# DeltaNet and a SiLU layer on one core: an earlier place for chunk 1's queries, a later one for three weight-narrowing steps

## The chip, the cores and the metric

The kernel runs on one core of one Trainium2 chip. The metric is the device time of one execution in microseconds (us). Five engines matter: PE multiplies matrices, DVE and ACT and POOL do elementwise work, and SP only issues DMAs. Each has its own stream of instructions; the streams meet through semaphores.

## The reference, cut to what matters

The input is a DeltaNet attention block (4 batches, 8 heads, 768 tokens, head size 48) followed by a SiLU layer with two weight matrices, 384 x 2048 and 2048 x 384.

```python
k_n = k / (norm(k) + 1e-6)
for t in range(768):
    y[:, :, t] = q[:, :, t] @ state                    # output reads the old state
    v_old = state.T @ k_n[:, :, t]
    state = state + beta[t] * outer(k_n[:, :, t], v[:, :, t] - v_old)
x = y.transpose(0, 2, 1, 3).reshape(3072, 384)
h = x @ w_in
out = (h / (1 + exp(-h))) @ w_out
```

The inputs come as 64-bit numbers; a float64 word arrives as two 32-bit words.

## The kernel before, in words

**Tiling.** The 768 tokens are cut into six chunks of 128, and each chunk into two halves of 64. Within a chunk the recurrence is solved as a small triangular system: `invert_first` inverts 16 x 16 corners of it on DVE for chunk 0, and the generator `joins(0)` then puts the corners together into 32 x 32 and 64 x 64 inverses with PE, in ten stages (`corner` twice, `turned` twice, `straight` and the first `merge_half` for each half of the batches, and the second `merge_half` twice). Each stage is a run of small matmuls into PSUM followed by copies of the result into SBUF, one half by ACT (`by_act`, L565) and one by DVE (`by_dve`, L568). After the stages `solve(0)` goes on with `inner` (L859), whose first result, `pz` of the first batch half, ACT copies into a slab in `sums_of_w`, and DVE copies into `z`. `first_outputs` (L905) multiplies from that slab.

**Weights.** The first weight matrix comes in eight pieces of 256 columns, 0 to 7. A piece is loaded as raw 64-bit words by `fetch_w_in` in three DMAs of 256 KB (L291), and is then narrowed to 32-bit floats by `narrow` in four instructions: two on ACT (L231, an Abs; L232, an Identity that rewrites the raw words in place), two on DVE (L236, L240), and an integer add on POOL (L244). A piece is a `Piece` object in a queue: `begin` issues its two ACT instructions; of the three counted steps of `fill`, the first issues nothing more, the second L236, the third L240 and L244. `begin_next` begins the first piece of the queue that has not begun, if its load has been issued.

**What sets the order.** The order on each engine is written out by hand: `pin` ties every instruction to the one before it on its engine. `joins` takes a list `between` with one entry for each of its ten stages, which is called when that stage has been issued; `none` does nothing, `sized` issues a POOL multiply and begins piece 1, `filled(n)` is n steps of `fill`. After the ten stages a script of letters is read: `s` is the next step of `solve`, `f` one step of `fill`, `b` is `begin_next`, `T` and `q` turn one batch of chunk 1's keys or queries with PE (`turn`, L521, which copies them to `stage` with ACT, L531 and L535), `j` goes on with the second half's stages, `r` runs one step of the SiLU layer (`hidden`, L1068).

**Loads.** All loads of this stretch are issued by SP, in the order of `in_line`. `pace` makes the next DMA wait for a given instruction. `deep` makes each DMA of a group wait for the one issued two before it to have landed, so that two are under way. An entry of `pace` takes the place of the `deep` wait for the DMA that it is put on. Chunk 1's queries (`load_q(1)`) are six DMAs, two of 192 KB and four of 96 KB (L142), into the tile `sums_of_g`; pieces 2 to 5 are loaded into `w_outs`, which the second weights take over later.

The entry `fetched`, called when the second `corner` stage has been issued, sends off the loads of this stretch:

```python
linked(fetch_w_in, 2, of=pins[seen_on])   # pace on the last DVE instruction so far (L743)
deep(load_q, 1)
for i in (3, 4, 5, 6):
    deep(fetch_w_in, i)
```

Of the kernel before, what the change touches and what calls it, by code (L numbers as in the profile page):

```python
# [19 lines left out]
def kernel(  # L20
# [11 lines left out]
    B, H, S, D = q.shape  # L32
# [8 lines left out]
    T = 32  # L41
# [36 lines left out]
    pins = {}  # L78

    def pin(op):  # L80

        engine = op.ins.engine
        if engine in pins:
            behind(op, pins[engine])
        pins[engine] = op
        return op

    line, pace, depth = [], [], []
# [21 lines left out]
    def together(*parts):  # L110
        for _ in zip_longest(*parts):
            pass
# [58 lines left out]
    def linked(fetch, *args, of=None):  # L171

        pace.append(of or line[-1])
        fetch(*args)

    def deep(fetch, *args):

        depth.append(True)
        fetch(*args)
        depth.pop()  # L180
# [22 lines left out]
    seen_on = pin(nc.vector.memset(seen[:], 0.0)).ins.engine  # L203
# [9 lines left out]
    for e in range(2):  # L213
        for g in range(2):
            to, of = slice(HH * e + HH // 2 * g, HH * e + HH // 2 * (g + 1)), slice(HH // 2 * g, HH // 2 * (g + 1))
# [596 lines left out]
    def merge_half(g, hf, second):  # L812

        y = ys[0][:, g]
        pms = [bank(room, "px" if second else "py") for room in (A, CC)]
        for i in range(HH // 2):
            for e in range(2):
                n, k = 2 * i + e, hf ^ e ^ g
                even, odd = slice(W * k, W * k + T), slice(W * k + T, W * (k + 1))
                if second:  # L820
                    to, left, right = even, y[odd, n, :], xis[g][odd, n, T:W]
                else:
                    left = aps[0, g][0][even, n // H, n % H, T:W]
                    to, right = odd, xes[0][even, g * HH + n, :]
                yield pin(nc.tensor.matmul(
                    pms[k][to, T * i : T * (i + 1)], lhsT=left, rhs=right, start=True, stop=True
                ))
        for k, by in enumerate((by_act, by_dve)):
            e, half = hf ^ k ^ g, slice(W * k, W * k + T) if second else slice(W * k + T, W * (k + 1))
            of = pms[k][half, 0 : HH // 2 * T].rearrange("p (h t) -> p h t", t=T)  # L830
            by(xis[g][half, e::2, T:W] if second else y[half, e::2, :], of)
# [442 lines left out]
    def fill(n):  # L1274

        for _ in range(n):
            if not queue:
                return
            piece = queue[0]
            piece.begin()  # L1280
            piece.done += 1
            if piece.done > 1:
                next(piece.steps)
            if piece.done == 3:
                narrowed.append(piece.name)
                queue.popleft()
                for i in freed:
                    fetch_w_out(i)
                freed[:] = {
                    ("in", 4): [0], ("in", 5): [1], ("in", 7): [4], ("out", 2): [5], ("out", 3): [6], ("out", 4): [7]  # L1290
                }.get(piece.name, [])
                if eager and queue and queue[0].name in raws:
                    soon.append(queue[0])
            elif eager and piece.done == 1 and len(queue) > 1 and queue[1].name in raws:
                soon.append(queue[1])
# [108 lines left out]
    def joins(hf, between=()):  # L1404

        for stage in (
            corner(0, hf), corner(1, hf), turned(0, hf), turned(1, hf), straight(0, hf), merge_half(0, hf, False),
            straight(1, hf), merge_half(1, hf, False), merge_half(0, hf, True), merge_half(1, hf, True),
        ):
            yield from stage  # L1410
            for what in between[:1]:
                for one in what if isinstance(what, tuple) else (what,):
                    one()
            between = between[1:]
# [4 lines left out]
    def filled(n):  # L1419
        return lambda: fill(n)  # L1420

    def fetched():
        linked(fetch_w_in, 2, of=pins[seen_on])
        deep(load_q, 1)
        for i in (3, 4, 5, 6):
            deep(fetch_w_in, i)

    def sized():
# [3 lines left out]
    def none():  # L1432
        pass

    together(joins(0, [none, fetched, none, sized, filled(2), none, filled(1), none, begin_next, none]))

    pieces = chained(hidden(0, 0), hidden(0, 1), project())

# [132 lines left out]
                pieces = chained(feed_forward(1, 0), feed_forward(1, 1))  # L1571

    for text in (
        "s f s f T f q T s q T j5 j4 j8 j8 f j5 f q r T j20 j5 j8 j4 j16 j5 j4 b r q r f j4 j4 f W7 r b j4 f2 j4 j4 j32 r f e j6 j6 b j8 j4 f j4 j20 f j4 r j4 j99 l h f2 b l s w2 f r2 l p r s l w3 r p r l p f l2 f l3 b l f l2 s l f l p l3 r l3 s l f l r l2 p f s2 l2 H f l4 f r2 f p2 v l g G r i p i p r2 f i i2 r i r i b l i r f r i r b r2 i b b b i2 r2 i2 f b i5 r6 f r f r i2 r2 f r i r f r f i4 f i b r2 i3 b f b f r i r i f k r f r z i b r s r2 t z s b r2 b s m2 r5 t f t m f t m2 r s t m r b s b m r m2 s r m r m r c m2 s m r m t b m2 s m2 b m f m2 t r t m3 r m s m",
    ):
        script(text)
    for c in range(1, NCH):
# [59 lines left out]
```

## Time and profile before

| what | before |
|---|---|
| median of three runs | 641.72 us (639.18 to 643.24) |
| the profiled execution's own time | 639.7 us |
| its span | 638.0 us |
| PE busy | 621.5 us, 97% of the span |
| DVE, ACT, POOL busy | 399.1, 216.7, 94.2 us |
| mean granted PE clock | 0.986 |

The span is the time between the first and the last instruction of the profiled execution; 1.7 us of its own time lie around it. Where the profile says "idle before <- X", X is the thing that came last of what the instruction waited for. The granted clock is the share of full speed that the chip gave to PE. A row of SP's timeline is the issue of DMAs, not their movement; a DMA's landing is told in the landing summaries, or by the next issue that waited for it.

### The profile page before, as it was taken

To read this page: it belongs to the slowest core of one execution; us is meant where nothing else is said; L and a number is where in the kernel's file an instruction comes from. 1 tells how busy PE (TensorE), PEld (TensorE's weight loads), DVE (VectorE), ACT (ScalarE), POOL (GpSimd) and SP (SyncE) were. 2 spreads that over 40 slices of the span, in tenths; PEclk is the share of its full clock that TensorE was granted. 3 is DMA by queue.
4 is the path that set the end of the run, shared out by engine and by line. 5 is a ranking of instruction groups with operands and counts; after the bars stand their busy time and mean duration, and the time that the engine had idled before them with its cause. 6 is when DMAs were issued, how large, how long until landed. Compare 5 with 4: busy or idle time off the path is not lost.

```text
span 638.0 us, 21886 instructions
## 1 busy us (share of the span) xinstructions
PE 621.5 (97%) x9650; PEld 547.8 (86%) x9650; DVE 399.1 (63%) x902; ACT 216.7 (34%) x510; POOL 94.2 (15%) x95
## 2 busy tenths in 40 slices
PE   8789999999999999999999999999999999999997
PEld 5678788666789989989989989989999989989997
DVE  6855879998765975654976564986564964212112
ACT  3565665152251122451122451122451122441110
POOL 5423531246010020020020010020001000000000
PEclk9968999999999999999999999999999999999999
DMA  7845554160459242369242259233173033100101
GB/s 152 182 124 179 179 128 100 52 149 3 102 120 163 57 89 24 83 126 147 39 107 29 69 122 160 56 88 37 43 142 72 19 83 34 39 15 1 26 0 26
DMA packets 141694, 53.68 MB, mean 84 GB/s; under 512 B 113296, under 2 KB 135056, under 8 KB 141600
## 3 DMA queue, kind: packets, MB, share of 16 engines
q1 hardware_dynamic: 141120, 51.62, 39.6%
q8 instruction: 76, 1.25, 0.9%
q10 hardware_dynamic: 480, 0.67, 0.3%
q14 instruction: 18, 0.15, 0.1%
HBM read 39.62 MB, written 10.49 MB: 79 GB/s over the span
## 4 chain that ended last, share of the span: by engine, by line
PE 95%; DVE 3%; issue 1%; POOL 0%; ACT 0%; DVEq 0%; POOLq 0%
PE phid L1068 40%; PE px L1175 17%; PE py L1175 13%; PE po L1103 7%; PE pa L550 3%; PE pz L859 2%; PE ph L847 2%; PE pyc L940 2%; PE pyc L927 2%; PE pu L879 2%; PE pt L521 1%; PE px L801 1%; PE py L801 1%; PE pw L349 1%; PE pl L752 1%
## 5 line engine op out<-in xcount | busy, mean ns | idle before, releaser
L1068 PE MATMUL phid<-xT,w_in 128*128 128x256 f32 x1152 | 258.7, 383 | 0.1
L1068 PEld LDWEIGHTS phid<-xT,w_in 128*128 128x128 f32 x1152 | 217.1, 191 | 30.6 <-issue 1.0
L1078 ACT ACTIVATE gT<-phid 128x512 f32<-128x512 f32 x88 | 52.6, 598 | 145.0 <-PE phid L1068 140.7
L648 DVE SCALAR_TENSOR_TENSOR rank<-g,step,x 128x31 f32<-128x31 f32 (+15 forms) x124 | 49.7, 401 | 35.8 <-DMA g<-blocks 32.4
L1157 DVE TENSOR_TENSOR sums_of_g<-gT 128x384 f32<-128x384 f32 (+1 forms) x60 | 29.7, 514 | 56.5 <-ACT gT L1078 45.9
L1175 PE MATMUL py<-w_out,sums_of_g 128*128 128x192 f32 x320 | 56.8, 329 | 0.0
L1175 PE MATMUL px<-sums_of_w,sums_of_g 128*128 128x192 f32 x320 | 56.6, 329 | 0.0
L1175 PEld LDWEIGHTS px<-sums_of_w,sums_of_g 128*128 128x128 f32 x320 | 52.2, 190 | 0.5
L1175 PEld LDWEIGHTS py<-w_out,sums_of_g 128*128 128x128 f32 x320 | 52.2, 190 | 0.4
L653 DVE TENSOR_TENSOR x<-x,rank 128x31 f32<-128x31 f32 (+15 forms) x124 | 42.5, 343 | 4.3
L488 POOL TENSOR_TENSOR vf<-vf,n_slot 128x768 f32<-128x768 f32 x10 | 15.2, 1538 | 168.4 <-DMA vf<-in_v_dram 168.4
L886 DVE TENSOR_TENSOR state<-state,pu 48x384 f32<-48x384 f32 x44 | 24.3, 552 | 23.2 <-PE pu L879 22.3
L565 ACT COPY xT<-pyc 48x128 f32<-48x128 f32 (+2 forms) x120 | 31.2, 260 | 1.6
L509 DVE STREAM_TRANSPOSE kq<-stage 128x512 f32<-128x512 f32 x28 | 28.3, 1114 | 3.6 <-DMA stage<-in_q_dram 3.5
L1175 PE MATMUL py<-w_out,gT 128*128 128x192 f32 x160 | 28.4, 329 | 0.0
L1175 PE MATMUL px<-sums_of_w,gT 128*128 128x192 f32 x160 | 28.4, 329 | 0.0
L1175 PE MATMUL px<-w_out,gT 128*128 128x192 f32 x160 | 28.0, 327 | 0.0
L859 PEld LDWEIGHTS pz<-vf,xi 64*64 64x64 f32 x768 | 25.1, 142 | 3.2 <-issue 2.2
L571 POOL COPY g<-x 64x256 f32<-64x256 f32 x4 | 5.0, 1247 | 152.3 <-DVE x L656 152.3
L1175 PEld LDWEIGHTS px<-w_out,gT 128*128 128x128 f32 x160 | 26.4, 190 | 0.5
L859 PE MATMUL pz<-vf,xi 64*64 64x48 f32 x768 | 26.8, 226 | 0.0
L1175 PEld LDWEIGHTS py<-w_out,gT 128*128 128x128 f32 x160 | 26.1, 190 | 0.3
(202 smaller groups left out, 827.7 us busy)
## 6 DMA issues: line engine op xcount, KB each, us to landing
vf<-in_v_dram SPq DMA_DIRECT2D x48, 96.0 KB, 2.7
out_dram<-o SPq DMA_DIRECT2D x42, 96.0 KB, 2.2
w_out<-in_moe_w_in_dram SPq DMA_DIRECT2D x12, 256.0 KB, 3.3
sums_of_w<-in_moe_w_out_dram SPq DMA_DIRECT2D x8, 384.0 KB, 3.7
blocks<-ap SPq DMA_DIRECT2D x40, 64.0 KB, 1.9
kb<-in_k_dram SPq DMA_DIRECT2D x12, 192.0 KB, 4.4
kb<-in_k_dram SPq DMA_DIRECT2D x24, 96.0 KB, 4.6
raw<-in_moe_w_in_dram SPq DMA_DIRECT2D x9, 256.0 KB, 3.5
```

What stands on the lines that cost most here:

```text
L509: pin(nc.vector.transpose(out=kqs[c, b][:, :, j, :].rearrange("p a (i m) -> p a m i", i=T), in_=src.rearrange("p a (m d) -> p a m d", d=D) ...
L550: pin(nc.tensor.matmul(pa[e][half, p * n * W : (p + 1) * n * W], lhsT=kq[rows, p, 0, half], rhs=kq[rows, p, js[0] : js[-1] + 1, half], sta ...
L565: return pin(nc.scalar.copy(to, of))
L648: pin(nc.vector.scalar_tensor_tensor(out=tv, in0=g[:, 0:m, m : m + 1].to_broadcast([P, m, n]), scalar=step[:, m : m + 1], in1=x[:, m : m + ...
L653: yield pin(nc.vector.tensor_tensor(out=x[:, 0:m, m:T], in0=x[:, 0:m, m:T], in1=tv, op=ALU.add))
L859: yield pin(nc.tensor.matmul(pz[rows, n * D : (n + 1) * D], lhsT=xis[g][rows, u * H + 2 * p + e, :], rhs=vfs[c][rows, hf, g * HB + u, p, : ...
L886: pin(nc.vector.tensor_tensor(out=to, in0=to, in1=by_heads(pu[of]), op=ALU.add))
L1068: pin(nc.tensor.matmul(ph[:, j * GT : (j + 1) * GT], lhsT=w_in[:, a, (2 * f + j) * P : (2 * f + j + 1) * P], rhs=xTs[c, hf][:, a, :], star ...
L1078: pin(nc.scalar.activation(out=hidden_of(c, hf, f), in_=ph[:], func=ACTF.Silu, scale=-0.5 if in_blocks(c) else 0.5))
L1103: pin(nc.tensor.matmul(pos[i][:, 0:DM], lhsT=hidden_of(0, hf, f // 2)[:, at : at + C], rhs=w_outs[f // HFF][:, f % HFF, :], start=(f == 0) ...
L1157: pin(nc.vector.tensor_tensor(out=sums_of_g[:, k, fs], in0=of[0], in1=of[1], op=op))
L1175: pin(nc.tensor.matmul(to, lhsT=at, rhs=quarter(f, *b) if isinstance(b, tuple) else sums_of_w[b][:, f], start=start and f == 0, stop=f == ...
```

## The change: what it does

In `fetched`, chunk 1's queries are issued first, with the pace on the same DVE instruction, and piece 2 behind them as the first of the `deep` pieces. In the list of `joins(0)`, the third step of `fill` for piece 0 (L240 on DVE, L244 on POOL) goes from behind the second `straight` stage to behind the last stage, and `begin_next`, which there begins piece 2 (L231 and L232 on ACT), leaves the list. It comes back as a `b` at the head of the script, ahead of the first step of `solve(0)`.

```diff
     def fetched():
-        linked(fetch_w_in, 2, of=pins[seen_on])
+        pace.append(pins[seen_on])
         deep(load_q, 1)
-        for i in (3, 4, 5, 6):
+        for i in (2, 3, 4, 5, 6):
             deep(fetch_w_in, i)
...
-    together(joins(0, [none, fetched, none, sized, filled(2), none, filled(1), none, begin_next, none]))
+    together(joins(0, [none, fetched, none, sized, filled(2), none, none, none, none, filled(1)]))
...
     for text in (
-        "s f s f T f q T s q T j5 ...
+        "b s f s f T f q T s q T j5 ...
```

More of the change, by code (lines that the diff above doesn't have):

```diff
@@ L1573 @@
     for text in (
-        "s f s f T f q T s q T j5 j4 j8 j8 f j5 f q r T j20 j5 j8 j4 j16 j5 j4 b r q r f j4 j4 f W7 r b j4 f2 j4 j4 j32 r f e j6 j6 b j8 j4 f j4 j20 f j4 r j4 j99 l h f2 b l s w2 f r2 l p r s l w3 r p r l p f l2 f l3 b l f l2 s l f l p l3 r l3 s l f l r l2 p f s2 l2 H f l4 f r2 f p2 v l g G r i p i p r2 f i i2 r i r i b l i r f r i r b r2 i b b b i2 r2 i2 f b i5 r6 f r f r i2 r2 f r i r f r f i4 f i b r2 i3 b f b f r i r i f k r f r z i b r s r2 t z s b r2 b s m2 r5 t f t m f t m2 r s t m r b s b m r m2 s r m r m r c m2 s m r m t b m2 s m2 b m f m2 t r t m3 r m s m",
+        "b s f s f T f q T s q T j5 j4 j8 j8 f j5 f q r T j20 j5 j8 j4 j16 j5 j4 b r q r f j4 j4 f W7 r b j4 f2 j4 j4 j32 r f e j6 j6 b j8 j4 f j4 j20 f j4 r j4 j99 l h f2 b l s w2 f r2 l p r s l w3 r p r l p f l2 f l3 b l f l2 s l f l p l3 r l3 s l f l r l2 p f s2 l2 H f l4 f r2 f p2 v l g G r i p i p r2 f i i2 r i r i b l i r f r i r b r2 i b b b i2 r2 i2 f b i5 r6 f r f r i2 r2 f r i r f r f i4 f i b r2 i3 b f b f r i r i f k r f r z i b r s r2 t z s b r2 b s m2 r5 t f t m f t m2 r s t m r b s b m r m2 s r m r m r c m2 s m r m t b m2 s m2 b m f m2 t r t m3 r m s m",
     ):
```

## The prediction

> **What bounds the kernel now.** I read the page first, then the windows, to see where PE is not busy.
>
> ```profile
> span 638.0 us, 21886 instructions
> ...
> PE 621.5 (97%) x9650; PEld 547.8 (86%) x9650; DVE 399.1 (63%) x902; ACT 216.7 (34%) x510; POOL 94.2 (15%) x95
> ...
> PE 95%; DVE 3%; issue 1%; POOL 0%; ACT 0%; DVEq 0%; POOLq 0%
> ```
> ```profile
> 26.00:43.00 17.00, 12.72 (x514) 12.02 (x518) 9.57 (x18) 8.22 (x16) 8.72 (x7) 0.61 0.60 156
> ...
> 160.00:200.00 40.00, 38.28 (x583) 31.99 (x582) 23.60 (x58) 14.55 (x39) 4.02 (x4) 1.00 0.59 122
> 200.00:300.00 100.00, 100.00 (x1472) 92.52 (x1471) 67.14 (x163) 29.53 (x76) 8.44 (x9) 1.00 0.52 91
> ```
>
> In a row of windows the columns are the stretch, its length, busy us of PE, PEld, DVE, ACT and POOL, the granted clock, the DMA share and GB/s. PE is the bound: 621.5 of 638.0 us, 95% of the chain, and full from 200 to 300. The edit lies in 26 to 48 us, where PE is busy for 12.72 of 17.00 us in the first stretch and has a granted clock of 0.61. What PE loses there comes back only from later idle time, and there is little: 1.72 us in 160 to 200, none in 200 to 300. So the question is how much later or earlier PE leaves this stretch.
>
> The chain of waits in this stretch, and then ACT, DVE and PE in order of time:
>
> ```profile
> 36.33 0.43 DVE xi L568
> ...
> 36.79 0.96 DVE w_in L240
> ...
> 37.78 0.44 DVE xe_y L568
> ...
> 38.60 1.06 PE px L825 x31
> 39.67 3.47 PE pz L859 x62
> ```
> ```profile
> 37.58 0.88 ACT L231 ACTIVATE w_in<-w_out 128x768 f32<-128x768 f32 x1
> 38.37 0.97 ACT L232 ACTIVATE w_out<-w_out,plus 128x768 int32<-128x768 uint32 x1
> 39.70 0.36 ACT L565 COPY xi<-px 32x256 f32<-32x256 f32 x1 [0.37 <-PE px L825]
> 41.64 0.48 ACT L565 COPY sums_of_w<-pz 128x384 f32<-128x384 f32 x1 [1.58 <-PE pz L859]
> ```
> ```profile
> 42.16 0.56 DVE L568 COPY z<-pz 128x384 f32<-128x384 f32 x1 [2.09 <-ACT sums_of_w L565]
> ...
> 43.01 1.14 PE L905 MATMUL py<-ap,sums_of_w 64*64 64x64 f32 x46
> ...
> 44.57 0.60 PE L521 MATMUL pt<-ident,sums_of_g 128*128 128x128 f32 x4
> ```
>
> Piece 0's L240 (0.96 us) stands in the chain, between two DVE copies of the joins: that is a real delay. Piece 2's two ACT steps run from 37.58 to 39.34, 1.76 us, and have not waited for their data. After the joins, PE's `first_outputs` (L905) starts at 43.01 from the slab that ACT's copy at 41.64 writes.
>
> **The change part by part.**
>
> *Piece 0's L240 and L244 behind the joins.* DVE no longer holds the `xe_y` copy: it can follow the `xi` copies at 36.8 instead of 37.78, so the last `px` matmuls and all behind them come 0.96 us earlier. L240 and POOL's add then run from about 39, when DVE is idle (2.09 us before 42.16). Their result is needed by the first `hidden` matmuls, which stand behind all of L905 and most of the eight turns of chunk 1: these hide them, and without that cover they would cost their own time. Worth -0.96 us, if nothing else gates `first_outputs`. ACT's copies lose nothing by L244, and POOL has nothing else queued there.
>
> *The loads.* SP's issues, one row each (start, duration of the issue):
>
> ```profile
> 27.41 0.44 SPq L291 DMA_DIRECT2D raw<-in_moe_w_in_dram  x1
> 29.22 0.81 SPq L291 DMA_DIRECT2D w_out<-in_moe_w_in_dram  x2
> 33.37 0.38 SPq L142 DMA_DIRECT2D sums_of_g<-in_q_dram  x1
> 33.98 0.61 SPq L142 DMA_DIRECT2D sums_of_g<-in_q_dram  x1
> 36.57 0.60 SPq L142 DMA_DIRECT2D sums_of_g<-in_q_dram  x1
> 37.27 0.58 SPq L142 DMA_DIRECT2D sums_of_g<-in_q_dram  x1
> 39.55 0.60 SPq L142 DMA_DIRECT2D sums_of_g<-in_q_dram  x1
> 40.38 1.44 SPq L142 DMA_DIRECT2D sums_of_g<-in_q_dram  x1
> 42.62 0.35 SPq L291 DMA_DIRECT2D w_out<-in_moe_w_in_dram  x1
> 43.82 0.35 SPq L291 DMA_DIRECT2D w_out<-in_moe_w_in_dram  x1
> 45.96 0.33 SPq L291 DMA_DIRECT2D w_out<-in_moe_w_in_dram  x1
> 48.01 0.33 SPq L291 DMA_DIRECT2D w_out<-in_moe_w_in_dram  x1
> 48.64 0.33 SPq L291 DMA_DIRECT2D w_out<-in_moe_w_in_dram  x1
> ```
> ```profile
> DMA to landing us min/median/max: 3.7/4.1/4.4
> ```
>
> The last row is the landing summary of pieces 1 and 2 (15 to 30 us). Because of `deep`, each issue from 36.57 on starts when the one two rows above it has landed (33.98 and 33.37 wait in the same way for piece 2). So this table holds landings: the queries and piece 3 form two ladders, 33.37, 36.57, 39.55, 42.62, 45.96, 48.64 (steps 3.20, 2.98, 3.07, 3.34, 2.68) and 33.98, 37.27, 40.38, 43.82, 48.01 (3.29, 3.11, 3.44, 4.19). Piece 3 is complete at 48.64, 15.27 us after the first query.
>
> In the changed kernel the same two ladders are climbed by the same sizes, with piece 2 in the place of piece 3. The first query is issued at 29.22, where the pace lets go. That gives piece 2 at 29.22 + 15.27 = **44.5**. But the second query now waits for piece 1's last DMA, which was issued at 27.41 and takes up to 4.4 us: 31.8. From there the odd ladder ends at 31.8 + 14.03 = **45.9**. I take 45.2, between the two, and keep 44.5 and 46.5 as ends. Before, piece 2's three DMAs were issued together from 29.22 and landed, by the 3.7 to 4.4 us, near 34. It is now some 11 us later.
>
> The queries arrive four us earlier, but PE first reads them at 44.57, without a wait, and the first half of them (three DMAs) had landed at 39.55 by the ladder. I count this gain as nothing. Pieces 3 to 6, twelve DMAs queued behind piece 2 on SP, land about 2 us later than before (44.5 and the 6.0 us from 42.62 to 48.64 for one more piece, against 48.64); they are begun by `b`, `f` and `r` words that stand behind PE's work, which moves by more. POOL issues no DMA here.
>
> *Piece 2's ACT steps ahead of `solve(0)`.* Here is the new wait. `b` puts L231 and L232 on ACT ahead of the copies of `inner`, and L231 reads piece 2. That ACT really stands still for such a load, the view of waits shows for other pieces:
>
> ```profile
> ACT w_out L231 <- DMA sums_of_w<-in_moe_w_out_dram: 12.4, 2, 7.5
> ```
>
> Twice ACT waited, 7.5 us the longer time. Queued behind it on ACT are the slab copy of `pz` (41.64 before), the `z` copy of the other half, the `xT` copy and the copies of chunk 1's turns. DVE's `z` copy waits for the slab copy (42.16, 2.09 idle), and PE's L905 needs the slab. So PE goes on when piece 2 has landed (45.2), Abs and Identity are through (+1.76), the slab is copied (+0.48), and three hand-overs are paid (about 0.15 in all): **47.6**, against 43.01. That is +4.6 us (3.9 to 5.9 by the ends of the landing). The 0.96 us gained above only makes PE's stop longer, from about 42.1 to 47.6: it is not in the sum.
>
> *PE's clock.* Windows of one step of the granted clock:
>
> ```profile
> 36.70:40.11 3.41, 2.34 (x64) 2.01 (x62) 2.29 (x5) 2.75 (x5) 1.85 (x1) 0.50 0.47 91
> 40.11:43.53 3.42, 3.42 (x82) 3.42 (x82) 0.72 (x2) 0.48 (x1) 0.00 (x0) 0.50 0.31 58
> 43.53:46.94 3.41, 3.41 (x102) 3.11 (x96) 2.45 (x4) 2.78 (x6) 0.00 (x0) 1.00 0.50 157
> 50.35:53.77 3.42, 3.06 (x127) 2.88 (x127) 2.50 (x6) 1.68 (x4) 0.00 (x0) 1.00 0.34 105
> 53.77:57.18 3.41, 3.41 (x11) 2.77 (x10) 0.28 (x1) 2.16 (x4) 1.83 (x1) 0.50 0.53 181
> ```
> ```profile
> L521 PE MATMUL pt<-ident,sums_of_g 128*128 128x128 f32 x4 | 1.1, 421 | 0.0
> ...
> L521 PE MATMUL pt<-ident,kb 128*128 128x128 f32 x16 | 2.5, 276 | 0.0
> ```
>
> A window with 2.34 us of PE work left the clock at 0.50; one full of work (40.11 to 43.53) was followed by 1.00. Before, the joins and `inner` paid for this return, and L905 started 0.5 us ahead of it. With a stop of 5.5 us in between the clock stays at 0.50 and PE must earn it again from 47.6. By the same grid it is full at 50.35 if the window that begins at 46.94 counts, after 2.75 us, or at 53.77, after 6.2 us. The two groups above are four turns in 1.1 us at the half clock (53.9 to 57.1) and sixteen in 2.5 at the full one (43.6 to 50.3), 0.275 against 0.156 us each: 0.43 of the time at half clock is lost. So the return costs 0.43 x 2.75 = 1.2 to 0.43 x 6.2 = 2.7 us, less 0.2 for the 0.5 us that were slow before: +1.0 to +2.5. I take **+1.7**, the middle, as the grid's phase need not be that of this execution. The Trainium skill ("TensorE: Matmul & The Clock Gate", What's actually happening) gives the return as a fixed 3.4 us of sustained work; by it this term would be an estimated 1.3 and the forecast 647.6. It also ties the loss of the clock to an idle window, which the row 50.35:53.77 does not bear out: 3.06 of 3.42 us busy, and the next window stands at 0.50.
>
> *The sum.* 4.6 + 1.7 = +6.3 us on the profiled execution: 639.7 + 6.3 = 646.0. That execution is near the lower end of the runs shown (639.18 to 643.24), so I put the sum on their median: 641.72 + 6.3 = **648.0 us**.
>
> **The rivals.** The bound between "same" and "slower" is 1%, 6.4 us, about what a measurement of this kernel can tell from no change; the forecast lies on it.
>
> *Part of it comes back, or is shorter* (0.22). Piece 2 lands at 44.5, the clock returns in the first window (+3.9 + 1.0), and idle time behind it (1.72 us in 160 to 200) takes all it can: +3.2, 644.9, or 644 to 646 with what one set of runs differs from another. For it: the 1.72 exists. Against it: nothing shows that this idle time hangs on anything but PE's own results.
>
> *Two slow windows and a late piece* (0.15). Landing at 46.5 and the clock at 53.77 or one window behind it: 5.9 + 2.5 + up to 1.5, 650 to 652.
>
> *Piece 2 is in time* (0.05), the other side. The price is set by one point: piece 2's landing against 38.7, when ACT would have copied the last `px`. Ahead of it, ACT's 1.76 us end at 40.5, just when `pz` is ready (41.64 less 0.96), and L240's 0.96 us is all that moves: 641.0 at best. It needs nine DMAs in 9.5 us from 29.22, where the ladder took 15.27; the shortest step in it is 2.68, so even five such steps end at 42.6.
>
> *The change does not do what it says* (0.03): if the order on ACT were not that of the script, and the slab copy went ahead of piece 2's Abs, the result is the one above.
>
> **How the numbers follow.** The forecast's own range, 646 to 650, holds 0.55; the rivals have 0.22, 0.15, and 0.08 for the two last. To hold 8 in 10 I reach from 644.0 to 651.5. Faster by over 1% is 0.02: no case gives it but an error. Over 1% slower (above 648.1) are the rival with two slow windows and a bit over half of the forecast: 0.47. The rest, 0.51, lies within 1%.
>
> **What would show it.** ACT's L231 of piece 2 has the longest wait of the stretch, about 5 us, released by the DMA of `w_out`; L905 starts at 46.7 to 48.9; ACT's slab copy follows L232 at once; PE's idle time before L905 is 4.5 to 6.5 us; the granted clock is 0.50 for 2.7 us or more behind it; the `px` matmuls of the second batch half start near 37.3. From 100 us on all is as before, only later, and 200 to 300 stays full. The prediction is wrong if L231 does not wait, if the queries take less than 2 us a step, or if PE is back at its old distance to the end by 200 us.

## The result, and the profile after

The changed kernel takes 647.73 us in the median of six runs (646.64 to 649.0), the kernel before 641.29 us beside it (639.18 to 643.57): a ratio of 1.0098, 95% interval 1.0069 to 1.0126. Two more sets of runs on other occasions gave 1.0076 (1.0046 to 1.0106) and 1.0072 (1.0049 to 1.0096). It is slower by some 0.7 to 1.0%, about 5 us.

The page of the changed kernel: its span, the engines' busy time, and the chain that ended last.

```profile
span 645.9 us, 21886 instructions
...
PE 623.7 (97%) x9650; PEld 548.7 (85%) x9650; DVE 397.8 (62%) x902; ACT 216.7 (34%) x510; POOL 93.8 (15%) x95
...
PE 89%; DMA 6%; DVE 2%; ACT 1%; issue 1%; POOL 0%; SPq 0%; DVEq 0%; POOLq 0%
```

The span grew by 7.9 us, PE's busy time by 2.2. The rest, 5.7 us, is PE standing idle. And a new thing has come into the chain: DMA, 6%, which had no share before. The windows of the changed kernel tell where PE lost the time:

```profile
26.00:43.00 17.00, 11.90 (x494) 10.85 (x492) 9.74 (x18) 7.37 (x15) 8.24 (x7) 0.64 0.61 139
43.00:60.00 17.00, 11.69 (x284) 10.33 (x282) 4.99 (x9) 7.58 (x13) 3.01 (x2) 0.66 0.52 161
```
In the kernel before, the second of these windows reads:
```profile
43.00:60.00 17.00, 16.64 (x358) 14.14 (x354) 9.25 (x15) 8.72 (x16) 3.69 (x2) 0.88 0.50 160
```

Of the new idle time 4.95 us lie between 43 and 60 us (17.00 - 11.69 against 17.00 - 16.64), and the granted clock there is 0.66 in place of 0.88. ACT, and then PE, of the changed kernel in order of time:

```profile
40.82 0.36 ACT L565 COPY xi<-px 32x256 f32<-32x256 f32 x1 [1.76 <-PE px L825]
47.28 0.89 ACT L231 ACTIVATE w_in<-w_out 128x768 f32<-128x768 f32 x1 [6.10 <-DMA w_out<-in_moe_w_in_dram]
48.07 0.96 ACT L232 ACTIVATE w_out<-w_out,plus 128x768 int32<-128x768 uint32 x1
48.92 0.47 ACT L565 COPY sums_of_w<-pz 128x384 f32<-128x384 f32 x1
```
```profile
39.73 1.06 PE L825 MATMUL px<-xi,xe_y 32*32 32x32 f32 x31 [0.81 <-issue]
40.71 3.65 PE L859 MATMUL pz<-vf,xi 64*64 64x48 f32 x64
49.44 1.56 PE L905 MATMUL py<-ap,sums_of_w 64*64 64x64 f32 x48 [5.08 <-ACT sums_of_w L565]
```

ACT waits 6.10 us for piece 2, runs Abs and Identity, and only then copies the slab; PE stands still for 5.08 us and starts L905 at 49.44, where the kernel before had it at 43.01. The chain of the changed kernel in the same stretch shows the ladder of loads, each row one DMA from its issue to its landing:

```profile
29.95 4.63 DMA sums_of_g<-in_q_dram
...
34.65 2.73 DMA sums_of_g<-in_q_dram
...
37.40 3.31 DMA sums_of_g<-in_q_dram
...
40.73 3.58 DMA w_out<-in_moe_w_in_dram
...
44.32 2.85 DMA w_out<-in_moe_w_in_dram
```

Three queries and two parts of piece 2, one behind the other, end at 47.17; ACT goes on at 47.28. The 6% are not all this wait: in this execution the chain follows the loads on, through the later pieces to 67.56 us, and from there by ACT to PE at 73.57, where PE waits for only 0.21 us. In two more profiles of the changed kernel the chain leaves the loads at piece 2, for ACT's L231, and DMA has 4%.

### The profile page after: what moved, and what is told of

Same layout as the page of the kernel before. It is cut to its first block, busy times and chain, and to the rows that moved or that the text cites. A ratio compares the mean times of both kernels' runs of the same rounds, so it can differ in the third digit from the quotient of the medians.

```text
span 645.9 us, 21886 instructions
## 1 busy us (share of the span) xinstructions
PE 623.7 (97%) x9650; PEld 548.7 (85%) x9650; DVE 397.8 (62%) x902; ACT 216.7 (34%) x510; POOL 93.8 (15%) x95
## 4 chain that ended last, share of the span: by engine, by line
PE 89%; DMA 6%; DVE 2%; ACT 1%; issue 1%; POOL 0%; SPq 0%; DVEq 0%; POOLq 0%
PE phid L1068 38%; PE px L1175 17%; PE py L1175 12%; PE po L1103 7%; PE pa L550 3%; DMA w_out<-in_moe_w_in_dram 3%; PE pz L859 2%; PE ph L847 2%; DMA sums_of_g<-in_q_dram 2%; PE pyc L940 2%; PE pu L879 2%; PE pyc L927 2%; PE px L801 1%; PE py L801 1%; PE pw L349 1%
## 5 line engine op out<-in xcount | busy, mean ns | idle before, releaser
L1068 PE MATMUL phid<-xT,w_in 128*128 128x256 f32 x1152 | 258.3, 382 | 1.0 <-issue 0.7
L1068 PEld LDWEIGHTS phid<-xT,w_in 128*128 128x128 f32 x1152 | 216.0, 190 | 32.2 <-issue 3.2
L488 POOL TENSOR_TENSOR vf<-vf,n_slot 128x768 f32<-128x768 f32 x10 | 15.0, 1509 | 170.4 <-DVE sums_of_g L1157 49.9
L859 PEld LDWEIGHTS pz<-vf,xi 64*64 64x64 f32 x768 | 25.0, 142 | 3.2 <-issue 2.6
L859 PE MATMUL pz<-vf,xi 64*64 64x48 f32 x768 | 26.6, 226 | 0.0
```

What stands on the lines that cost most here:

```text
L859: yield pin(nc.tensor.matmul(pz[rows, n * D : (n + 1) * D], lhsT=xis[g][rows, u * H + 2 * p + e, :], rhs=vfs[c][rows, hf, g * HB + u, p, : ...
L1068: pin(nc.tensor.matmul(ph[:, j * GT : (j + 1) * GT], lhsT=w_in[:, a, (2 * f + j) * P : (2 * f + j + 1) * P], rhs=xTs[c, hf][:, a, :], star ...
```

## The experiments

**The steps moved, the loads in their old order.** On the changed kernel:

```diff
     def fetched():
-        pace.append(pins[seen_on])
+        linked(fetch_w_in, 2, of=pins[seen_on])
         deep(load_q, 1)
-        for i in (2, 3, 4, 5, 6):
+        for i in (3, 4, 5, 6):
```

> The steps moved as in the changed kernel, the loads in the old order (piece 2 ahead of the queries). Theory, the stop is ACT's wait for piece 2: the piece lands near 34 us, so ACT's L231 of piece 2 waits for nothing behind the last px copy, L905 starts near 42.2 us, and the time is 640.3 to 641.3 us (0 to 1 us under before, for L240 gone from the chain). Rival, the later places of the steps cost by themselves (piece 0's add and piece 2's steps late for the first hidden matmuls): L905 near 42, but 643 us or more, with PE waiting ahead of its first L1068.

Measured: 642.68 us against 642.43 beside it, ratio 1.0007 (0.9984 to 1.0030). ACT and PE of its profile:

```profile
42.47 0.36 ACT L565 COPY xi<-px 32x256 f32<-32x256 f32 x1 [2.30 <-PE px L825]
42.74 0.90 ACT L231 ACTIVATE w_in<-w_out 128x768 f32<-128x768 f32 x1
...
41.37 1.06 PE L825 MATMUL px<-xi,xe_y 32*32 32x32 f32 x31 [1.35 <-issue]
```

L231 follows the copy without a wait, and the loss is gone: the new places of the steps do not cost by themselves. But the gain that I had expected from L240 is not seen either; an interval that reaches down to 0.9984 could just hold its 0.96 us. PE's second `px` stage is preceded by 1.35 us in which it waited for nothing that the profile shows, as it is in the changed kernel (0.81 above). The last experiment below takes this up.

**The loads moved, the steps in their old places.** On the kernel before: `fetched` as in the changed kernel, the list of `joins(0)` and the script as they were.

> The loads moved as in the changed kernel, the steps in their old places. Theory: L231 of piece 2 now stands ahead of the last px copy on ACT and waits there until the piece lands, 45 to 47.5 us; then 1.76 us, that copy, the second batch half of inner, so L905 starts near 51 us, later than in the changed kernel; 648 to 651 us. Rival, only the new places of the steps cost: 641 to 642 us, as before.

Measured: 647.77 us, ratio 1.0079 (1.0051 to 1.0107). ACT, then PE:

```profile
47.91 0.89 ACT L231 ACTIVATE w_in<-w_out 128x768 f32<-128x768 f32 x1 [9.09 <-DMA w_out<-in_moe_w_in_dram]
...
49.96 1.83 PE L859 MATMUL pz<-vf,xi 64*64 64x48 f32 x29 [6.77 <-ACT xi L565]
...
51.65 1.55 PE L905 MATMUL py<-ap,sums_of_w 64*64 64x64 f32 x45
```

The wait stands one copy further ahead, as it had to, and L905 starts at 51.65. The order of the loads alone brings the loss. That it would be larger than the changed kernel's is not borne out: the two ratios cannot be told apart.

**Piece 2 begun later.** The changed kernel without the `b` at the head of the script; the first `fill` step that comes to piece 2 begins it.

```diff
-        "b s f s f T f q T s q T j5 ...
+        "s f s f T f q T s q T j5 ...
```

> The changed kernel without the b at the head of the script: piece 2's two ACT steps are issued by the first fill step that comes to it, behind the slab and xT copies. Theory: no ACT wait ahead of the slab copy, L905 near 42.2 us, the clock back at about 43.5 us, 640.3 to 641.5 us with the queries still loaded first. Rival, the order of the loads costs by itself (later pieces late, DMA queues): 644 us or more.

Measured: 643.42 us, ratio 1.0014 (0.9989 to 1.0039). Its ACT copies the slab at once, and PE goes on:

```profile
42.49 0.48 ACT L565 COPY sums_of_w<-pz 128x384 f32<-128x384 f32 x1 [1.58 <-PE pz L859]
...
43.85 1.48 PE L905 MATMUL py<-ap,sums_of_w 64*64 64x64 f32 x46
```

With the queries still loaded first and piece 2 still late, the loss is gone: what costs is that ACT waits for the piece ahead of PE's next operand. Nor do the earlier queries gain anything.

**The wait behind the two `inner` stages.** The changed kernel with `b` one word later, `"s b f s f T ..."`, so that ACT copies the slab and the other half of `z` first.

> The changed kernel with the b one word later, behind the two inner stages: ACT copies the slab and the other half of z first, and waits for piece 2 ahead of the xT copy. Theory (what counts is which PE work stands behind ACT's wait): L905 starts at 43 to 46 us; PE goes on through the first outputs and three turns, and stops at the second L905 group for want of a free bank, until ACT is through at about 48.5; the stop is 2 to 4 us and the time 2 to 4.5 us over the kernel before (644 to 647 us), under the changed kernel. Rival (any wait of ACT for piece 2 costs the same): the changed kernel's time.

Measured: 644.95 us, ratio 1.0037 (1.0005 to 1.0069), the changed kernel beside it 1.0072. ACT, then PE:

```profile
46.92 0.92 ACT L231 ACTIVATE w_in<-w_out 128x768 f32<-128x768 f32 x1 [0.20 <-DMA w_out<-in_moe_w_in_dram]
...
49.12 0.33 PE L905 MATMUL py<-ap,sums_of_w 64*64 64x64 f32 x2 [0.88 <-ACT xT L565]
```

ACT's wait shrinks to 0.20 us, since the copies ahead of it fill the time, and PE's first L905 group runs at 45.28; the second waits for the `xT` copy. The ratio has about half of the loss; the medians stand closer, 3.6 us above the kernel before against 5.3 for the changed kernel, and the interval leaves anything from almost none of the loss to all of it. So the rival, that any wait of ACT for piece 2 costs the same, is not shut out by the times. The stop in this profile is shorter than the 2 to 4 us that I had expected, but the profiled execution took 641.03 us, one of the shortest of twelve that spread from 640.89 to 649.32: what the long ones lost is not shown.

**The ladder taken away.** The changed kernel, with the six queries and piece 2 issued without `deep`:

```diff
         pace.append(pins[seen_on])
-        deep(load_q, 1)
-        for i in (2, 3, 4, 5, 6):
+        load_q(1)
+        fetch_w_in(2)
+        for i in (3, 4, 5, 6):
             deep(fetch_w_in, i)
```

> The changed kernel, but the six queries and the three DMAs of piece 2 are issued without waiting for the one two before (deep is taken from both; pieces 3 to 6 keep it). Theory, the ladder of landings is what makes piece 2 late: all nine are issued by about 36.5 us, piece 2 lands at 38.5 to 40.5, ACT's wait at L231 is under 1 us, L905 starts at 42.5 to 44 and the time is within 2 us of the kernel before. Rival, the queries' many small descriptors fill the DMA engines and piece 2 is as late without the ladder: landing beyond 44, 645 us or more.

Measured: 642.0 us, ratio 1.0000 (0.9976 to 1.0025). ACT has the piece when it comes to it:

```profile
42.55 0.36 ACT L565 COPY xi<-px 32x256 f32<-32x256 f32 x1 [2.58 <-PE px L825]
42.82 0.90 ACT L231 ACTIVATE w_in<-w_out 128x768 f32<-128x768 f32 x1
```

Both changes of order are still in this kernel; only the two-at-a-time issue of these nine loads is gone, and with it the loss. The queries ahead of piece 2 cost by the ladder and not by the DMA engines' time.

**PE kept busy in the stop.** The changed kernel with matmuls between `inner` and L905 whose results nobody reads, eight in the first kernel and five in the second:

```diff
+    def keep_warm(n):
+        pw = bank(CC, "pw")
+        CC.rotate(1)
+        for _ in range(n):
+            pin(nc.tensor.matmul(pw[:, 0:DM], lhsT=ident[:], rhs=states[0] ...
...
-        "b s f s f T ...
+        "b s x8 f s f T ...
```

> The changed kernel with eight more matmuls (128 x 384, results unused) on PE between inner and L905, where PE stands idle for some 5 us. Theory, the half clock behind the stop is the second term: L905 starts within 0.6 us of where it does in the changed kernel, but at a granted clock of 1.00 or within 2 us of it, and the time is 0.8 to 2.5 us under the changed kernel's (645.2 to 647.0 us). Rival, the stop is all and the clock costs nothing: the changed kernel's time within 0.5 us, 647.2 to 648.4.

Measured with eight: 651.73 us, ratio 1.0137 (1.0099 to 1.0175).

```profile
44.49 7.45 PE L1519 MATMUL pw<-state,ident 128*128 128x384 f32 x16
51.87 0.93 PE L905 MATMUL py<-ap,sums_of_w 64*64 64x64 f32 x48
```

Eight were too many: L905 starts two us after the slab was there (copied by 49.9), so this run does not tell the two theories apart. It does show L905 in 0.93 us at full clock, against 1.56 in the changed kernel. With five, and the changed kernel once more beside it:

> The changed kernel once more, beside the next two on one chip. Theory: 1.007 to 1.013 of the kernel before; L231 of piece 2 waits 5 to 7 us, L905 starts at 47.5 to 50 us, granted clock 0.50 from about 31 to 51 us or later.

> The changed kernel with five more matmuls (128 x 384, results unused) on PE in the stop between inner and L905; eight had run 7.45 us, over the end of the stop, so five should take about 4.7 us and end with it. Theory, the half clock behind the stop is the second term, 1.0 to 2.5 us: L905 starts as in the changed kernel, at full clock or within 2 us of it, and the time is 1.0 to 2.5 us under the changed kernel's of this chip. Rival, the clock costs nothing once the stop is there: the changed kernel's time within 0.6 us.

Measured: the changed kernel 645.95 us, ratio 1.0076 (1.0046 to 1.0106); with five matmuls 647.63, ratio 1.0091 (1.0063 to 1.0118). L905 starts at 49.44 at full clock, 0.7 us behind the slab copy (done at 48.7), and the time is not lower. A last pair with more rounds:

> The changed kernel, as the partner on one chip of the next two. 1.005 to 1.012 of the kernel before; in its profile L905 starts at 47.5 to 50 us.

> The changed kernel with five more matmuls on PE in the stop, as before, with more rounds. Theory one (the clock's return behind the stop is a term of the end): 1.0 to 2.5 us under the changed kernel of this chip, 0.2 to 0.4%. Theory two (what the slow return costs is given back within 20 us, because the second dip of the clock, which the kernel before and the kernel with five more matmuls both show some 10 us behind the return, is missing from the changed kernel): the changed kernel's time within 0.15%, and a second dip of 3.4 us in this profile and none in the changed kernel's.

Measured: the changed kernel 646.61 us, ratio 1.0072 (1.0049 to 1.0096); with five 648.9, ratio 1.0102 (1.0069 to 1.0136). In this execution the five matmuls ran over by 2.1 us (the slab was there at 48.9):

```profile
45.67 5.52 PE L1519 MATMUL pw<-state,ident 128*128 128x384 f32 x10
51.11 0.93 PE L905 MATMUL py<-ap,sums_of_w 64*64 64x64 f32 x48
```

The length of the stop and the clock differ from one execution to the next, so no fixed number of matmuls fills it. Neither theory is settled by this pair: the second dip of the clock that theory two asks for was in the profiles of the eight and of the first five, and was missing here. Less what the matmuls ran over, the filled kernels take as long as the changed kernel or up to about 1 us longer: no run shows a gain from the restored clock. That is a rough account, since the overrun is known of one execution of each, and the added matmuls also shift PE's stream, which the next experiment shows to move PE's stops. The section on the prediction comes back to it.

**The PE stream shifted.** The kernel before, with 24 small matmuls ahead of the first `corner` stage:

```diff
     for n in range(1 + Q):
         done = next(inv)
+        if n == 11:
+            small_ones(24)     # 32 x 32, from ident, results unused
```

> The kernel before with 24 small matmuls (32 x 32, results unused) on PE ahead of the first corner stage, where PE is idle for 0.97 us. In the profile these are 48 matmuls and 48 weight loads. Theory, PE's stops in the joins without a releaser (1.58 us ahead of all but 7 matmuls of the second straight stage, and the one at the second px stage, 256 PE instructions later) are PE's program being fetched in blocks of 256 instructions: they move 48 matmuls back in the stream, into the middle of stages, the first near the end of the first straight stage, the second 18 matmuls into the second py stage; time within 1 us of before. Rival, they are waits for ACT's or DVE's copies, L240 and piece 1's steps among them: they stay at the first matmuls of the second straight stage and of the second px stage.

Measured: 643.66 us in one run, 642.02 for the kernel before beside it. PE and then DVE of its profile, and two windows that run from stop to stop:

```profile
33.92 0.28 PE L765 MATMUL pl<-sums_of_w 32*32 32x32 f32 x5 [1.55 <-issue]
38.02 0.47 PE L825 MATMUL py<-xe_y,ap 32*32 32x32 f32 x10 [1.85 <-issue]
...
37.30 0.96 DVE L240 SCALAR_TENSOR_TENSOR w_in<-raw,w_in 128x768 uint32<-128x768 uint32 x1
```
```profile
29.35:33.90 4.55, 3.01 (x127) 2.83 (x127) 1.54 (x4) 2.33 (x4) 3.94 (x3) 0.57 0.82 264
33.93:38.00 4.07, 2.23 (x128) 2.10 (x127) 3.45 (x7) 1.95 (x6) 0.00 (x0) 0.50 0.48 107
```

The same in the kernel before, a row of PE and the two windows:

```profile
34.75 1.01 PE L765 MATMUL pl<-sums_of_w 32*32 32x32 f32 x57 [1.58 <-issue]
```
```profile
30.48:34.74 4.26, 2.69 (x128) 2.56 (x128) 2.40 (x5) 2.95 (x6) 2.39 (x2) 0.50 0.60 197
34.76:38.58 3.82, 2.78 (x128) 2.51 (x127) 2.58 (x5) 2.64 (x7) 0.69 (x1) 0.50 0.48 95
```

The stops went with the instruction stream. They now lie in the middle of stages, where no copy is waited for, and from one to the next it is 128 matmuls and 128 weight loads in both kernels (127 where a record is missing or lies on the border). And L240 ran from 37.30 to 38.26, three quarters of it inside a stop that ended at 38.02: here it delayed nobody. One run says nothing of this kernel's time; the places of the stops are what it was for.

## Why the prediction was right, and where it was not

This table puts the profiles side by side: where the L905 group starts, and the span from there to the end. Each row is one execution, and the executions of one kernel differ by 2 to 9 us, so a difference of one or two us between rows means little.

| kernel | L905 starts, us | span | from L905 to the end | ratio to before |
|---|---|---|---|---|
| before | 43.0 | 638.0 | 595.0 | 1 |
| steps only | 45.8 | 643.6 | 597.8 | 1.0007 |
| later begin | 43.9 | 643.1 | 599.2 | 1.0014 |
| not deep | 45.9 | 641.4 | 595.5 | 1.0000 |
| shifted stream | 43.5 | 641.9 | 598.4 | one run |
| b behind inner | 45.3 | 639.3 | 594.0 | 1.0037 |
| changed | 49.4 | 645.9 | 596.5 | 1.0098 |
| changed, second set | 48.2 | 644.2 | 596.0 | 1.0076 |
| changed, third set | 48.4 | 644.2 | 595.8 | 1.0072 |
| loads only | 51.7 | 647.9 | 596.2 | 1.0079 |

*The new wait: right, in place and in kind.* L231 of piece 2 waits for its load ahead of the slab copy, and L905 waits for that copy. Undoing any one part of the cause (the load order, the place of the begin, the ladder) takes the loss away.

*Its size: about right, with some luck.* L905 was forecast at 47.6, with 46.7 to 48.9 as the sign, and came at 49.4, 48.2 and 48.4. The steps of the ladder held: from the first query's landing (34.6) to the end of piece 2 the changed kernel took 12.6 us, where the old rows gave 12.07. What came later was its foot: the first query was issued 0.7 us later than reckoned and took 4.6 us where the old rows gave 3.2. In the profiled execution piece 1 was itself late, as ACT's wait for it shows,

```profile
34.04 0.89 ACT L231 ACTIVATE w_in<-raw 128x768 f32<-128x768 f32 x1 [2.02 <-DMA raw<-in_moe_w_in_dram]
```

and the second query waits for piece 1's last DMA: 5.2 us from issue to landing in the second set, where I had taken 4.4 at most. (By my own numbers the second ladder ends at 45.8, not 45.9; nothing hangs on it.) On the other side the 43.01 that I subtracted is the earliest L905 of all kernels without the stop; the six in the table average 44.6. The stop, as a difference of averages (48.7 against 44.6), is 4.1 us, where the forecast had 4.6: L905 came 1.1 us later than forecast, and was measured from a start 1.6 us too early, and the two misses cancel in part.

*L240 out of the chain, -0.96 us: wrong, and without effect on the sum.* The chain of waits named L240 as what the `xe_y` copy waited for, and I took the time behind it for free. In the changed kernel the copy comes 0.04 us behind the `xi` copies, and PE still starts the second `px` stage only at 39.73, after 0.81 us of "issue". PE's own stop stood right behind L240's delay and hid it. The sign that `px` of the second half would start near 37.3 failed with it. The forecast swallowed this gain in the longer stop, so the sum did not feel the mistake; my expectations for the two kernels with the steps moved and no stop did not have that cover: 640.3 to 641.5 us, where 642.7 and 643.4 came.

*The queries four us earlier, nothing: right.* The kernel with the later begin keeps them early and gains nothing. That the later pieces, queued behind piece 2, cost nothing was nearly right too: in the profiled execution the chain runs through them, but PE waits for 0.21 us.

*The clock, +1.7 us: the cost is there at first, and is not shown at the end.* The changed kernel's windows, in the stretch at half clock and behind it:

```profile
31.00:54.70 23.70, 14.87 (x438) 13.80 (x437) 8.62 (x16) 9.85 (x19) 5.24 (x4) 0.50 0.51 140
54.70:58.11 3.41, 3.41 (x98) 3.03 (x94) 1.16 (x2) 2.15 (x4) 1.01 (x1) 1.00 0.53 165
```

The clock stays at 0.50 from L905 to 54.70, 5.3 us, between the forecast's 2.75 and 6.2; in the other two profiles of the changed kernel it is 5.4 and 5.1 us. The first and the sixth group of L1068, before and then after:

```profile
48.55 1.46 PE L1068 MATMUL phid<-xT,w_in 128*128 128x256 f32 x6
...
65.65 1.56 PE L1068 MATMUL phid<-xT,w_in 128*128 128x256 f32 x6
```
```profile
57.14 1.46 PE L1068 MATMUL phid<-xT,w_in 128*128 128x256 f32 x6
...
71.31 1.56 PE L1068 MATMUL phid<-xT,w_in 128*128 128x256 f32 x6
```

L905 is 6.43 us later than before, the first L1068 8.59: the slow return costs 2.16 us, as the working said. But the sixth is 5.66 us later. The kernel before loses its clock a second time, at 53.77 to 57.18 (the row in the prediction), and the changed kernel, in all three of its profiles, does not. So this term was mis-sized: I counted the return behind the stop and left out that the kernel before, in the execution that I worked from, pays for a return of its own a little later.

What decides on this second loss can be read from the profiles. The granted clock changes in steps of 3.41 us, and a group of small matmuls (L736 and, behind it, L752), 2.9 us long, stands ahead of the second L1068. Where it starts, before and then after, and the changed kernel's windows of one step around it:

```profile
50.38 0.80 PE L736 MATMUL pl<-sums_of_w,ap 32*32 32x16 f32 x68
```
```profile
58.97 0.80 PE L736 MATMUL pl<-sums_of_w,ap 32*32 32x16 f32 x68
```
```profile
58.11:61.52 3.41, 3.06 (x125) 2.72 (x124) 1.71 (x5) 0.85 (x2) 0.00 (x0) 1.00 0.55 160
61.52:64.94 3.42, 3.42 (x30) 2.85 (x26) 1.08 (x2) 2.90 (x5) 1.85 (x1) 1.00 0.56 173
```

In the kernel before the group begins with a window (50.35), and the next window stands at 0.50. In the changed kernel it begins 0.86 us inside one, behind larger matmuls; PE is busy for the same 3.06 us, and the clock stays. This sorts all thirteen profiles. In the five with the second loss (before, later begin, not deep, eight matmuls, the first five matmuls) the group begins from 0.24 us ahead of a window to 0.19 us inside it; in the eight without it 0.85 to 1.95 us inside. The two executions with five matmuls, one kernel, fall on different sides: it is set by how the windows lie on the stream in an execution. The kernel before shifted by 24 small matmuls has no second loss either. So the loss in the profile that I worked from was an accident of that execution as much as a property of the kernel.

The other reading behind this term, that a window full of work is followed by the full clock, does not hold in general either. Two windows of the steps-only kernel:

```profile
42.25:45.66 3.41, 3.41 (x71) 3.35 (x67) 1.94 (x3) 2.42 (x4) 1.69 (x1) 0.50 0.46 88
45.66:49.07 3.41, 3.41 (x65) 3.29 (x62) 1.73 (x4) 1.54 (x3) 0.15 (x1) 0.50 0.62 183
```

The first is full, almost all of it with the matmuls of L859, and the clock comes only behind the second. The shifted kernel's full window from 40.21 to 43.62 us is followed by 0.50 too.

From L905 to the end the changed kernel's profiles take 595.8 to 596.5 us, inside what the kernels without the stop take (594.0 to 599.2), and the filled stops gained nothing. With three ratios that average 1.008, or 5.3 us, against the 4.1 us of the stop, a term of about one us may be left for the clock; that stays open, since the filled kernels ran over the end of the stop in all three profiles, by 0.7 to 2.1 us.

*The sum.* 6.3 us were forecast, 6.4, 3.9 and 5.3 us are the differences of the medians; that the first set comes within 0.1 us is luck, with one term 0.5 us too large and the other not shown. The forecast lay on the 1% line, and the measured ratios lie on it and below it. Of the rivals, piece 2 in time and an order on ACT other than the script's are out by L231's wait. Two slow windows and a late piece did describe the profiled execution up to L1068, but not its end. The rival in which part comes back is the one the later sets speak for, though by the clock and not by the idle time from 160 to 200 us, which is 1.72 us before and 1.51 after. (The prediction left out another 1.52 us of idle time, from 60 to 100 us; it is 1.59 after, so nothing came back there.)

## What to carry to other kernels

A step that reads a DMA belongs on its engine behind everything that another engine is about to need, or its load belongs ahead; moving the load and the step at once can make a wait of either. When loads go two at a time, here each step of two loads cost about 3 us (2.7 to 4.2 in the rows shown, but for a first step of 4.6 behind piece 1) whatever their size between 96 and 256 KB, so a load moved behind six others comes nine or ten us later. And before a row of the chain of waits is taken away on paper, ask what the next limit is: here PE's own stop stood right behind L240. A clock that falls or not by how its windows lie in an execution is to be read from several executions, not from one.

## What the runs showed of the hardware

PE's stops without a releaser in the joins come every 256 PE instructions, weight loads counted, and mostly last 0.8 to 2 us (the shortest in these profiles 0.45; the longest, 2.95, in the changed kernel, where piece 1 was late too). The queue table of the page has a row that fits:

```profile
q8 instruction: 76, 1.25, 0.9%
```

76 packets for 19,300 PE instructions are 254 to a packet, 16 KB each. I read the stops as PE's program arriving in blocks; that they are tied to the place in the stream is shown by the shifted kernel, that it is the fetch that ends them is inferred. The Trainium skill ("Runtime: NRT & Kernel Launch", Instruction fetch mechanics) has the program refilled in 16 KiB blocks of 256 instructions, with which the spacing agrees. It also says that the fetch is hidden by the rate at which instructions are issued. Here the measurement says otherwise: 128 small matmuls and their weight loads keep PE busy for 2.2 to 3.0 us, and a block takes 3.8 to 4.6 us from stop to stop. In the joins such a stop, and not a copy on ACT or DVE, is often what ends last.

The granted clock also fell where PE had been busy for 3.06 of 3.42 us (50.35 to 53.77 before), with small matmuls in most of that window; an idle window is not needed for it. Nor is busy time what decides: a window as busy (58.11 to 61.52 after, 3.06 us) left the clock at 1.00. At this place of the stream, over the thirteen profiles, larger matmuls fill 0 to 0.8 us of the windows that lost the clock and 0.85 to 1.95 us of those that kept it. Whether it is their share or their place at the head of the window that counts, no run tells.
